# Five of nine positions of a q batch turned by DMA instead of TensorE, with their scaled values kept in other tiles

## The chip, the cores and the metric

The kernel runs on one core of one Trainium2 chip. The metric is device microseconds for one execution. The time shown for a kernel is the median of several runs.

## What is computed

Linear attention with cosine weights, followed by a gated feed-forward block. Cut to what matters:

```python
# q, k, v: (8 batches, 8 heads, 576 tokens, 64)
theta = pi / 2 * pos / 576
def phi(x): r = maximum(x, 0); return concatenate([r * cos(theta), r * sin(theta)], -1)
q_p, k_p = phi(q), phi(k)                       # last axis 128 wide
kv  = einsum('bhsf,bhsd->bhfd', k_p, v)
den = einsum('bhsf,bhf->bhs', q_p, k_p.sum(axis=2))[..., None] + 1e-6
x   = einsum('bhsf,bhfd->bhsd', q_p, kv) / den  # then to (4608 tokens, 512)
out = (gelu(x @ w_gate) * (x @ w_val)) @ w_out  # 512 -> 1536 -> 512
```

## The kernel before

**Tiling.** Batches are of 576 tokens, blocks of the feed-forward part of 512; nine blocks of tokens cover the eight batches. While TensorE works on the feed-forward matmuls of one block, the other engines and short insertions in TensorE's stream prepare the attention of the next batches. The order of instructions is written out by hand: each engine executes its instructions in the order of the program, and semaphores are placed where data or a buffer requires it.

**One batch of attention.** A batch is loaded as `qf`, `kf`, `vf` tiles (float32, two buffers each): 128 partitions are 2 heads of a pair times 64 groups of tokens, and each partition holds, for the four head pairs m, nine consecutive tokens, the positions j = 0 to 8 (`R = 9`). `prep` (L153) applies relu and the cosine (VectorE, L163) or the sine (ScalarE, L161) for one position over all four pairs and writes bf16 into the tile `qp` or `kp`. These have one buffer each, so batch 2's `qp` overwrites batch 1's. `cast_v` (L178) makes v bf16. `kv_unit` (L236) forms kv with 72 matmuls. q has to stand with its 128 features on the partitions before it can be multiplied with kv; that is the tile `qT`, one buffer. It is made in one of two ways:

- `turn_q_pe` (L201) with `turn_j` (L702): one TensorE transpose (L205) for each head pair and position, into a PSUM bank, and a copy from there to `qT` (L707, on ScalarE or VectorE). Batches 0 and 1 take this way.
- `turn_q` (L192): two DMA transposes from SP's queue (L194), one for each half of the partitions, 64 x 4608 elements each. Batches 2 to 7 take this way.

`nm_unit` (L274) then makes, for 128 tokens (a row tile t of five: t = 0 reads positions 0 and 1, t = 1 reads 2 and 3, t = 2 reads 4 and 5, t = 3 reads 6 and 7, t = 4 reads 7 and 8), eight matmuls of `qT` with kv (L283), the reciprocal and the division on VectorE (L294 to L296), which give `x_sb`. That is turned again (`turn_x_pe`, L354, TensorE transposes L358 and a ScalarE copy L362; or `turn_x` with DMA transposes L350) into `xT`, the input of the next block.

**The stage of the change.** It comes after block 0's 12 gate-and-value units (`gv_unit`, L401, with gelu on ScalarE L409 and the product on VectorE L410). During the last three of these, q of batch 1 is scaled: positions 0-2, 3-5 and 6-8. Then the list `order` (L773) mixes the output matmuls of block 0 (`o_part`, L431; four rows of tokens in three parts of four matmuls, with a ScalarE copy L440 and a store L421 from SP's queue at the end of each row) with batch 1's attention: turning q, scaling k ("k"), casting v ("q8" does this after the last transposes), kv, and the numerators "nm" for t = 0 to 3. "q2" scales the first positions of batch 2's q, on ScalarE first and then VectorE. After the list come the loads of batch 3's q from SP's queue. t = 4 of batch 1 follows in block 1 (about 60.5 us).

**Queues.** GpSimd's queue carries the loads of weights and of batches 1 and 2, all issued by 44.3 us; SP's queue carries stores, later loads and DMA transposes. SP's queue is empty between the loads at the start and the first store, issued at 51.74 us.

**Later weight sums.** `wo_sum` (L451) makes four differences of w_out's blocks, `T1` to `T4`, each in a tile of its own of 1536 bf16 columns (L459, L460). VectorE makes the first at 66.3 us.

Of the kernel before, what the change touches and what calls it, by code (L numbers as in the profile page):

```python
# [10 lines left out]
BF16 = mybir.dt.bfloat16  # L11
# [5 lines left out]
def kernel(  # L17
# [15 lines left out]
    B, H, S, D = q.shape  # L33
    F = 2 * D
    C = H * D
    J = moe_w_gate.shape[1]
    CT = C // 128
    JT = J // 128
    NP = H // 2
    R = S // 64  # L40
# [9 lines left out]
    weights = ctx.enter_context(tc.tile_pool(name="weights", bufs=1))  # L50
    inp = ctx.enter_context(tc.tile_pool(name="inp", bufs=2))
    attn = ctx.enter_context(tc.tile_pool(name="attn", bufs=1))
# [12 lines left out]
    def bank(i):  # L65
        return ps[:, i]

    def bank16(i):
        return ps[:, i].bitcast(BF16)
# [6 lines left out]
    staged = {}  # L76
# [54 lines left out]
    vx_tiles = []  # L131
    for i in range(2):
        t = consts.tile([128, NP, R, D + 1], BF16, name=f"vx{i}")
# [9 lines left out]
    act_copy, dve_copy = nc.scalar.copy, nc.vector.tensor_copy  # L143


    phi = {}

    def phi_tile(name, b):
        if (name, b) not in phi:
            phi[name, b] = attn.tile([128, NP, R, F], BF16, name=name + "p")  # L150
        return phi[name, b]

    def prep(name, b, part, js, m0=0, m1=NP, eng=None):  # L153
        dst = phi_tile(name, b)
        src = staged[name, b]
        tab = (cos_t, sin_t)[part]
        for j in js:
            o = dst[:, m0:m1, j, part * D:(part + 1) * D]
            i = src[:, m0:m1, j * D:(j + 1) * D]
            if eng is nc.scalar:  # L160
                nc.scalar.activation(o, i, AF.Relu, scale=tab[:, j:j + 1])  # L161
            else:
                (eng or nc.vector).tensor_scalar(  # L163
                    o, i, 0.0, tab[:, j:j + 1], op0=ALU.max, op1=ALU.mult
                )

    def prep_run(name, b, part, m, j0=0, j1=R):
        dst, src = phi_tile(name, b), staged[name, b]
        tab = (cos_t, sin_t)[part]
        nc.vector.scalar_tensor_tensor(  # L170
            dst[:, m, j0:j1, part * D:(part + 1) * D],
            src[:, m, j0 * D:j1 * D].rearrange("p (j d) -> p j d", d=D),
            0.0,
            tab[:, j0:j1, None].to_broadcast([128, j1 - j0, D]),
            op0=ALU.max,
            op1=ALU.mult,
        )

    def cast_v(b, m0, m1, copy, j0=0, j1=R):
        copy(  # L180
            vx_tiles[b % 2][:, m0:m1, j0:j1, 0:D],
            staged["v", b][:, m0:m1, j0 * D:j1 * D].rearrange("p m (j d) -> p m j d", d=D),
        )

    qT = {}

    def qt_tile(b):
        if b not in qT:
            qT[b] = attn.tile([128, 2, NP, R * 64], BF16, name="qT")
        return qT[b]  # L190

    def turn_q(b):  # L192
        for i in range(2):
            nc.sync.dma_start_transpose(  # L194
                out=qt_tile(b)[:, i].rearrange("f m (j p) -> f (m j) p", p=64),
                in_=phi["q", b][64 * i:64 * i + 64].rearrange("p m j f -> p (m j f)"),
            )

    def q_cols(b, t, h):
        c0 = min(t * 128, S - 128)  # L200
        return qT[b][:, h % 2, h // 2, c0:c0 + 128]  # L201

    def turn_q_pe(b, m, js, dst):
        for n, j in enumerate(js):
            nc.tensor.transpose(  # L205
                out=dst[:, n * 128:(n + 1) * 128],
                in_=phi["q", b][:, m, j, :],
                identity=ident,
            )

    kv_sb = {}

    def kv_pairs(b, m0, m1, banks):
        kp, vx = phi["k", b], vx_tiles[b % 2]
        for m in range(m0, m1):
            for j in range(R):
                for i in range(2):
                    rr = slice(64 * i, 64 * i + 64)
                    nc.tensor.matmul(
                        bank(banks[i])[:, (m % 2) * (D + 1):(m % 2 + 1) * (D + 1)],  # L220
                        lhsT=kp[rr, m, j, :],
                        rhs=vx[rr, m, j, :],
                        start=(j == 0),
                        stop=(j == R - 1),
                    )
# [8 lines left out]
            )  # L234

    def kv_unit(b):  # L236
        kp, vx = phi["k", b], vx_tiles[b % 2]
        for m in range(NP):
            for j in range(R):
                for i in range(2):  # L240
                    rr = slice(64 * i, 64 * i + 64)
                    nc.tensor.matmul(  # L242
                        bank(6 + i)[:, m * (D + 1):(m + 1) * (D + 1)],
                        lhsT=kp[rr, m, j, :],
                        rhs=vx[rr, m, j, :],
                        start=(j == 0),
                        stop=(j == R - 1),
                    )
        kv_sb[b] = attn2.tile([128, NP, 2, D + 1], BF16, name="kv_sb")
        for i in range(2):  # L250
            nc.scalar.copy(
                kv_sb[b][:, :, i, :],
                bank(6 + i)[:, 0:NP * (D + 1)].rearrange("p (m d) -> p m d", m=NP),
            )
# [99 lines left out]
    def turn_x_pe(b, t, to, copy):  # L354
        x = xs.pop((b, t))
        p = bank16(to)[:, 0:CT * 128].rearrange("p (c n) -> p c n", c=CT)
        for ct in range(CT):
            nc.tensor.transpose(  # L358
                out=p[:, ct, :], in_=x[:, ct * 128:(ct + 1) * 128], identity=ident
            )  # L360
        for blk, c, o, m in pieces(b, t):
            copy(xT_block(blk)[:, :, c:c + m], p[:, :, o:o + m])  # L362
# [86 lines left out]
    JH, CH = JT // 2, C // 2  # L449
    ts = {}  # L450

    def wo_sum(name):
        if not ts:
            ts["B11"], ts["B12"] = wo_sb[:, 0:JH, 0:CH], wo_sb[:, 0:JH, CH:C]
            ts["B21"], ts["B22"] = wo_sb[:, JH:JT, 0:CH], wo_sb[:, JH:JT, CH:C]
        x, y = {
            "T1": ("B12", "B11"), "T2": ("B22", "T1"), "T3": ("B22", "B12"), "T4": ("T2", "B21"),
        }[name]
        ts[name] = weights.tile([128, JH, CH], BF16, name=name)  # L459
        nc.vector.tensor_tensor(ts[name], ts[x], ts[y], op=ALU.subtract)  # L460

    def h_parts(n, p):
# [239 lines left out]
    def turn_j(b, m0, m1, js, to, copy):  # L702

        n = len(js)
        for m in range(m0, m1):
            turn_q_pe(b, m, js, bank16(to)[:, (m - m0) * n * 128:])
        copy(  # L707
            qt_tile(b)[:, :, m0:m1, js[0] * 64:(js[0] + n) * 64].rearrange(
                "f i m (j p) -> f m j i p", j=n
            ),  # L710
            bank16(to)[:, 0:(m1 - m0) * n * 128].rearrange(
                "f (m j i p) -> f m j i p", m=m1 - m0, j=n, i=2
            ),
        )
# [44 lines left out]
    for jt in range(4, JT):  # L759
# [12 lines left out]
    banks0 = (4, 5, 0, 1)  # L772
    order = (  # L773
# [6 lines left out]
    )  # L780
    for what, *a in order:
        if what == "o":
            o_part(a[0], range(a[1], a[1] + 4), banks0[a[0]], act_copy)
        if what == "q":
            turn_j(1, a[0], a[1], range(a[2], a[2] + 4), a[3], (dve_copy, act_copy)[a[3] % 2])
        if what == "q8":
            turn_j(1, 0, 4, (R - 1,), a[0], dve_copy)
            for m in (0, 2):
                cast_v(1, m, m + 2, dve_copy)
        if what == "k":  # L790
            prep("k", 1, 0, range(R))
            prep("k", 1, 1, range(7), eng=nc.scalar)
            prep("k", 1, 1, range(7, R))
        if what == "q2":
            prep("q", 2, 1, range(*a), eng=nc.scalar)
            prep("q", 2, 0, range(*a))
        if what == "kv":
            kv_unit(1)
        if what == "nm":
            nm_unit(1, a[0], a[1])  # L800
        if what == "xt":
            turn_x_pe(1, a[0], a[1], act_copy)
# [74 lines left out]
    for n in range(1, NB - 2):  # L877
        b = n + 1
# [4 lines left out]
        for jt in range(min(JT, FAST - n * JT)):  # L883
# [6 lines left out]
            else:  # L890
                for i in range(2):
                    half, unit = divmod(2 * jt + i, heads)
                    gv_unit(n, unit, half * HALF, HALF)
                    if n == 1:
                        j = JA + 2 * jt + i
# [4 lines left out]
            if n > 1:  # L900
                p, u = divmod(jt, 6)
# [6 lines left out]
            if b < B:  # L908
# [12 lines left out]
                i = jt - t_nm - 1  # L921
# [22 lines left out]
                c = {(2, 1): 2}.get((n, jt), b if n > 1 and jt == t_turn else None)  # L944
# [22 lines left out]
    for t in range(UNITS):  # L967
        n, jt = divmod(FAST + t, JT)
        if n == NB - 1 and jt in (9, 10):
            h_sum(n, jt - 9, "S3", eng=nc.gpsimd)  # L970
        if n < NB - 2:
# [3 lines left out]
            a, j0 = (("S2", 0), ("S4", 0), ("S2", 512), ("S4", 512))[t]  # L975
# [23 lines left out]
    for what in (  # L999
# [3 lines left out]
        if isinstance(what, str):  # L1003
            p = "ST".index(what[0])
# [33 lines left out]
```

## Time and profile before

| | us |
|---|---|
| median of 3 runs | 312.69 (312.32 to 313.81) |
| the profiled execution | 312.79 |
| its span | 311.0 |
| TensorE busy in the span | 301.0 |
| VectorE busy | 246.8 |
| ScalarE busy | 186.6 |
| last gate-and-value matmuls of block 0 end | 39.5 |
| batch 1's kv product starts | 47.7 |
| batch 1's numerators t = 0, 1, 2, 3 start | 49.8, 50.9, 52.3, 53.6 |
| block 1's first gate-and-value matmuls start | 55.0 |

The span is the time from the first to the last instruction of the profiled execution; the execution's own time has some 1.8 us around it. Times of single instructions are from the span's start. In the profile PE is TensorE, DVE VectorE, ACT ScalarE, POOL GpSimd and SP the engine that issues most DMAs; "idle before" is the time in which the engine stood, with what ended it.

### The profile page before, as it was taken

What the parts mean: (1) busy time and instruction counts of PE and PEld (TensorE: products, weight loads), DVE (VectorE), ACT (ScalarE), POOL (GpSimd) and SP (SyncE); (2) the same over time, 40 slices, a digit from 0 to 9 for tenths busy, and PEclk for the clock granted to TensorE, in tenths of its full rate; (3) what the DMA queues carried; (4) which work ended last, traced back from release to release, by engine and by line L of the source; (5) the groups of instructions that cost most, each with busy time, mean ns of one, the idle gap of its engine ahead of it and who ended that gap; (6) DMA issues with size and microseconds to landing.
All of it is one profiled execution on the core that took longest, in us unless ns stands there. A gap on an engine that the chain in (4) does not pass through costs nothing.

```text
span 311.0 us, 7704 instructions
## 1 busy us (share of the span) xinstructions
PE 301.0 (97%) x2867; PEld 208.2 (67%) x2895; DVE 246.8 (79%) x622; ACT 186.6 (60%) x468; POOL 67.9 (22%) x70
## 2 busy tenths in 40 slices
PE   8889999999999999999999999999999999999993
PEld 3574456645876676666666566656668888888882
DVE  5954686699897997799688878899899787978782
ACT  7854685966564763365525932593328787787830
POOL 6775420000000000000000000000007991297310
PEclk9999999999999999999999999999999999999999
DMA  7999999971798956993898589538442111202034
GB/s 277 247 186 246 313 315 412 273 145 37 217 225 260 315 132 153 368 232 94 259 291 177 116 277 303 112 83 124 93 106 52 40 32 41 50 21 69 3 80 123
DMA packets 69077, 53.65 MB, mean 172 GB/s; under 512 B 45392, under 2 KB 54352, under 8 KB 69040
## 3 DMA queue, kind: packets, MB, share of 16 engines
q1 hardware_dynamic: 59264, 41.17, 52.0%
q0 software_dynamic: 9696, 11.93, 16.5%
q8 instruction: 22, 0.36, 0.5%
q14 instruction: 15, 0.12, 0.1%
q10 hardware_dynamic: 80, 0.07, 0.1%
HBM read 37.75 MB, written 9.44 MB: 152 GB/s over the span
## 4 chain that ended last, share of the span: by engine, by line
PE 87%; DMA 4%; issue 4%; POOL 2%; DVE 0%; SPq 0%; ACT 0%; POOLq 0%; ACTq 0%; DVEq 0%
PE ps L401 43%; PE ps L510 20%; PE ps L611 13%; PE ps L431 3%; PE ps L283 3%; PE ps L242 3%; DMA vf<-in_v_dram 2%; DMA wv_sb<-in_moe_w_val_dram 2%; POOL kf L494 1%; PE ps L373 1%; PE ps L205 1%; PE ps L358 0%; SPq L81 0%; POOL gate L679 0%; POOL wg_sb L95 0%
## 5 line engine op out<-in xcount | busy, mean ns | idle before, releaser
L401 PE MATMUL ps<-xT,wv_sb 128*128 128x512 bf16 (+1 forms) x338 | 80.6, 359 | 0.2
L401 PE MATMUL ps<-xT,wg_sb 128*128 128x512 bf16 (+1 forms) x326 | 79.5, 358 | 1.1 <-issue 0.3
L409 ACT ACTIVATE gel<-ps 128x512 f32<-128x512 f32 (+1 forms) x86 | 47.7, 556 | 46.5 <-PE ps L401 43.3
L410 DVE TENSOR_TENSOR hT<-gel,ps 128x512 bf16<-128x512 f32 (+1 forms) x86 | 54.0, 633 | 24.0 <-PE ps L401 19.2
L401 PEld LDWEIGHTS <-wv_sb 128*128 128x128 bf16 x344 | 33.6, 98 | 33.9
L401 PEld LDWEIGHTS <-wg_sb 128*128 128x128 bf16 x344 | 30.7, 98 | 20.9 <-issue 0.2
L974 POOL CAST gate<-qp 128x1 f32<-128x1 bf16 x1 | 0.2, 175 | 190.7 <-DVE qp L591 190.7
L510 PEld LDWEIGHTS <-S 128*128 128x128 bf16 x336 | 32.9, 98 | 10.9 <-DVE S L494 0.6
L528 ACT COPY u<-ps 128x256 f32<-128x256 f32 x42 | 15.6, 372 | 31.4 <-PE ps L510 30.8
L510 PE MATMUL ps<-T,S 128*128 128x256 bf16 x252 | 34.4, 273 | 0.0
L161 ACT ACTIVATE qp<-qf,sin_t 128x256 bf16<-128x256 f32 x72 | 32.1, 502 | 3.4 <-DMA qf<-in_q_dram 3.4
L510 PEld LDWEIGHTS <-hT 128*128 128x128 bf16 x288 | 28.2, 98 | 6.9
L524 DVE TENSOR_TENSOR o_sb<-u,ps 128x256 f32<-128x256 f32 x56 | 23.3, 416 | 10.5 <-ACT u L528 10.3
L161 ACT ACTIVATE kp<-kf,sin_t 128x256 bf16<-128x256 f32 (+1 forms) x73 | 30.0, 480 | 0.9 <-DMA kf<-in_k_dram 0.9
L296 DVE TENSOR_TENSOR x_sb<-ps,rec 128x512 bf16<-128x512 f32 x38 | 26.3, 691 | 1.8 <-DMA xT<-x_sb 0.6
L510 PE MATMUL ps<-wo_sb,hT 128*128 128x256 bf16 x192 | 23.7, 273 | 0.0
L163 DVE TENSOR_SCALAR qp<-qf,cos_t 128x256 bf16<-128x256 f32 x71 | 21.5, 350 | 2.3 <-DMA qf<-in_q_dram 2.3
L611 PE MATMUL ps<-qp,qf 128*128 128x256 bf16 x112 | 21.4, 273 | 0.1
L611 PE MATMUL ps<-xT,wg_sb 128*128 128x256 bf16 x112 | 21.4, 273 | 0.0
L163 DVE TENSOR_SCALAR kp<-kf,cos_t 128x256 bf16<-128x256 f32 x63 | 18.3, 347 | 0.0
L283 PEld LDWEIGHTS <-qT 128*128 128x128 bf16 x304 | 14.6, 98 | 2.7 <-ACT qT L707 0.3
L283 PE MATMUL ps<-kv_sb,qT 128*128 128x65 bf16 x304 | 16.0, 194 | 0.0
(121 smaller groups left out, 457.6 us busy)
## 6 DMA issues: line engine op xcount, KB each, us to landing
out_dram<-o_sb SPq DMA_DIRECT2D x69, 128.0 KB, 2.5
kf<-in_k_dram SPq DMA_DIRECT2D x12, 576.0 KB, 7.2
vf<-in_v_dram SPq DMA_DIRECT2D x12, 576.0 KB, 9.0
qf<-in_q_dram SPq DMA_DIRECT2D x10, 576.0 KB, 5.2
qf<-in_q_dram POOLq DMA_DIRECT2D x4, 576.0 KB, 12.1
kf<-in_k_dram POOLq DMA_DIRECT2D x4, 576.0 KB, 12.8
vf<-in_v_dram POOLq DMA_DIRECT2D x4, 576.0 KB, 12.9
wg_sb<-in_moe_w_gate_dram POOLq DMA_DIRECT2D x6, 256.0 KB, 6.9
```

The costliest lines, as they stand in the source:

```text
L161: nc.scalar.activation(o, i, AF.Relu, scale=tab[:, j:j + 1])
L163: (eng or nc.vector).tensor_scalar(o, i, 0.0, tab[:, j:j + 1], op0=ALU.max, op1=ALU.mult)
L242: nc.tensor.matmul(bank(6 + i)[:, m * (D + 1):(m + 1) * (D + 1)], lhsT=kp[rr, m, j, :], rhs=vx[rr, m, j, :], start=(j == 0), stop=(j == R ...
L283: nc.tensor.matmul(bank(b0 + h // 4)[:, (h % 4) * (D + 1):(h % 4 + 1) * (D + 1)], lhsT=q_cols(b, t, h), rhs=kv_sb[b][:, h // 2, h % 2, :], ...
L296: nc.vector.tensor_tensor(x, nm[:, :, :, 0:D], rec[:, :, :, None].to_broadcast([128, 2, 4, D]), op=ALU.mult,)
L401: nc.tensor.matmul(bank(b0 + g)[:, 0:w], lhsT=wt[:, ct, js], rhs=xt[:, ct, c0:c0 + w], start=(ct == 0), stop=(ct == CT - 1),)
L409: nc.scalar.activation(gel[:, 0:w], bank(b0)[:, 0:w], AF.Gelu)
L410: nc.vector.tensor_mul(hT[n][:, jt, c0:c0 + w], gel[:, 0:w], bank(b0 + 1)[:, 0:w])
L510: nc.tensor.matmul(at, lhsT=hs.setdefault(key, h_parts(n, p))[a][:, j], rhs=ts[b][:, j], start=(j == 0 and i in (1, 2, 4, 5)), stop=(j == ...
L524: nc.vector.tensor_tensor(o, got[key, k], x, op=op)
L528: nc.scalar.copy(got[key, i], at)
L611: nc.tensor.matmul(at(i, t), lhsT=wa[a][:, ct, jt * 128:(jt + 1) * 128], rhs=xb[n][b][:, ct], start=(ct == 0 and i in (1, 5)), stop=(ct == ...
```

## The change

Positions 4 to 8 of batch 1's q leave the TensorE way. Their scaled values no longer go to `qp` but into two extra tiles: positions 4 and 5 into one with the name `T1`, positions 6 to 8 into one with the name `T2`, so that they take the places in which two of w_out's differences are made later. Four DMA transposes (two halves for each of the two parts) are issued from SP's queue ahead of the list; 20 TensorE transposes and three copies leave it. Batch 1's `qT` is laid out in three parts (positions 0-3, 4-5, 6-8), so that each transfer writes one run. The casts of v stand in the list where the last transposes stood, and one of the two halves goes to ScalarE. The diff, cut to its core:

```diff
+    JB, JC = 4, 6
+    def parted(flat, n, b, name="q"):
+        ends = (0, JB, JC, R) if (name, b) == ("q", 1) else (0, R)
+        return [
+            (j0, flat[:, j0 * NP * n:j1 * NP * n].rearrange(
+                "p (m j n) -> p m j n", m=NP, j=j1 - j0))
+            for j0, j1 in zip(ends, ends[1:])
+        ]
+    def at_j(parts, j):
+        j0, t = [part for part in parts if part[0] <= j][-1]
+        return t, j - j0
     def phi_tile(name, b):
         if (name, b) not in phi:
-            phi[name, b] = attn.tile([128, NP, R, F], BF16, name=name + "p")
+            t = attn.tile([128, NP, R, F], BF16, name=name + "p")
+            phi[name, b] = parted(t.rearrange("p m j f -> p (m j f)"), F, b, name)
+            if (name, b) == ("q", 1):
+                for i, (j0, j1) in enumerate(((JB, JC), (JC, R))):
+                    t = weights.tile([128, JT // 2 * C // 2], BF16, name=f"T{i + 1}")
+                    phi[name, b][1 + i] = j0, t[:, 0:NP * (j1 - j0) * F].rearrange(
+                        "p (m j f) -> p m j f", m=NP, j=j1 - j0
+                    )
...
-    def turn_q(b):
+    def turn_q(b, part=0):
         for i in range(2):
             nc.sync.dma_start_transpose(
-                out=qt_tile(b)[:, i].rearrange("f m (j p) -> f (m j) p", p=64),
-                in_=phi["q", b][64 * i:64 * i + 64].rearrange("p m j f -> p (m j f)"),
+                out=qt_tile(b)[i][part][1].rearrange("f m j p -> f (m j) p"),
+                in_=phi["q", b][part][1][64 * i:64 * i + 64].rearrange("p m j f -> p (m j f)"),
             )
     def q_cols(b, t, h):
-        c0 = min(t * 128, S - 128)
-        return qT[b][:, h % 2, h // 2, c0:c0 + 128]
+        cols, j = at_j(qT[b][h % 2], min(2 * t, R - 2))
+        return cols[:, h // 2, j:j + 2].rearrange("f j p -> f (j p)")
...
     order = (
         [("q", 0, 2, 0, 6), ("q", 2, 4, 0, 7), ("o", 0, 0), ("k",), ("o", 1, 0)]
-        + [("q", 0, 2, 4, 2), ("o", 2, 0), ("q", 2, 4, 4, 3), ("o", 3, 0), ("o", 0, 4)]
-        + [("q8", 2), ("o", 1, 4), ("o", 2, 4), ("kv",), ("q2", 0, 2), ("o", 3, 4)]
+        + [("o", 2, 0), ("o", 3, 0), ("o", 0, 4)]
+        + [("v",), ("o", 1, 4), ("o", 2, 4), ("kv",), ("q2", 0, 2), ("o", 3, 4)]
...
+    turn_q(1, 1)
+    turn_q(1, 2)
     for what, *a in order:
...
-        if what == "q8":
-            turn_j(1, 0, 4, (R - 1,), a[0], dve_copy)
-            for m in (0, 2):
-                cast_v(1, m, m + 2, dve_copy)
+        if what == "v":
+            for m, copy in ((0, dve_copy), (2, act_copy)):
+                cast_v(1, m, m + 2, copy)
```

More of the change, by code (lines that the diff above doesn't have):

```diff
@@ L157, in prep @@
         for j in js:
-            o = dst[:, m0:m1, j, part * D:(part + 1) * D]
+            t, jj = at_j(dst, j)
+            o = t[:, m0:m1, jj, part * D:(part + 1) * D]
             i = src[:, m0:m1, j * D:(j + 1) * D]
@@ L167, in prep_run @@
     def prep_run(name, b, part, m, j0=0, j1=R):
-        dst, src = phi_tile(name, b), staged[name, b]
+        (_, dst), = phi_tile(name, b)
+        src = staged[name, b]
         tab = (cos_t, sin_t)[part]
@@ L183, in cast_v @@
         )
-    qT = {}
+    qT, first = {}, {}
     def qt_tile(b):
         if b not in qT:
-            qT[b] = attn.tile([128, 2, NP, R * 64], BF16, name="qT")
+            t = attn.tile([128, 2, NP * R * 64], BF16, name="qT")
+            qT[b] = [parted(t[:, i], 64, b) for i in range(2)]
+            n = qT[b][0][0][1].shape[2]
+            first[b] = t[:, :, 0:NP * n * 64].rearrange(
+                "f i (m j p) -> f i m j p", m=NP, j=n
+            )
         return qT[b]
-    def turn_q(b):
+    def turn_q(b, part=0):
         for i in range(2):
             nc.sync.dma_start_transpose(
-                out=qt_tile(b)[:, i].rearrange("f m (j p) -> f (m j) p", p=64),
-                in_=phi["q", b][64 * i:64 * i + 64].rearrange("p m j f -> p (m j f)"),
+                out=qt_tile(b)[i][part][1].rearrange("f m j p -> f (m j) p"),
+                in_=phi["q", b][part][1][64 * i:64 * i + 64].rearrange("p m j f -> p (m j f)"),
             )
     def q_cols(b, t, h):
-        c0 = min(t * 128, S - 128)
-        return qT[b][:, h % 2, h // 2, c0:c0 + 128]
+        cols, j = at_j(qT[b][h % 2], min(2 * t, R - 2))
+        return cols[:, h // 2, j:j + 2].rearrange("f j p -> f (j p)")
     def turn_q_pe(b, m, js, dst):
@@ L206, in turn_q_pe @@
                 out=dst[:, n * 128:(n + 1) * 128],
-                in_=phi["q", b][:, m, j, :],
+                in_=phi["q", b][0][1][:, m, j, :],
                 identity=ident,
@@ L213, in kv_pairs @@
     def kv_pairs(b, m0, m1, banks):
-        kp, vx = phi["k", b], vx_tiles[b % 2]
+        kp, vx = phi["k", b][0][1], vx_tiles[b % 2]
         for m in range(m0, m1):
@@ L236, in kv_unit @@
     def kv_unit(b):
-        kp, vx = phi["k", b], vx_tiles[b % 2]
+        kp, vx = phi["k", b][0][1], vx_tiles[b % 2]
         for m in range(NP):
@@ L458, in wo_sum @@
         }[name]
-        ts[name] = weights.tile([128, JH, CH], BF16, name=name)
+        t = weights.tile([128, JH * CH], BF16, name=name)
+        ts[name] = t.rearrange("p (j c) -> p j c", j=JH)
         nc.vector.tensor_tensor(ts[name], ts[x], ts[y], op=ALU.subtract)
@@ L706, in turn_j @@
             turn_q_pe(b, m, js, bank16(to)[:, (m - m0) * n * 128:])
+        qt_tile(b)
         copy(
-            qt_tile(b)[:, :, m0:m1, js[0] * 64:(js[0] + n) * 64].rearrange(
-                "f i m (j p) -> f m j i p", j=n
-            ),
+            first[b][:, :, m0:m1, js[0]:js[0] + n].rearrange("f i m j p -> f m j i p"),
             bank16(to)[:, 0:(m1 - m0) * n * 128].rearrange(
```

## The prediction

> **What bounds the kernel now.** I read the page first, then the TensorE timeline around the change, then ScalarE and VectorE in the same stretch, then the DMA queues.
>
> ```profile
> PE 301.0 (97%) x2867; PEld 208.2 (67%) x2895; DVE 246.8 (79%) x622; ACT 186.6 (60%) x468; POOL 67.9 (22%) x70
> ...
> DMA  7999999971798956993898589538442111202034
> ```
>
> TensorE is busy 97% of the span, and the chain that ended last is 87% TensorE. So what leaves its stream in front of the end shortens the kernel, and a wait put into that stream lengthens it. The second line is the mean busy share of the DMA engines in slices of 7.8 us: 9 tenths from 8 to 62 us. The change sits at 39 to 54 us, inside that full stretch.
>
> ```profile
> 39.52 1.06 PE L205 MATMUL ps<-ident,qp 128*128 128x128 bf16 x16
> ...
> 42.14 0.61 PE L205 MATMUL ps<-ident,qp 128*128 128x128 bf16 x8
> ...
> 43.45 0.61 PE L205 MATMUL ps<-ident,qp 128*128 128x128 bf16 x8
> ...
> 45.62 0.39 PE L205 MATMUL ps<-ident,qp 128*128 128x128 bf16 x4
> ...
> 47.67 1.33 PE L242 MATMUL ps<-vx,kp 64*128 64x65 bf16 x72
> ...
> 52.05 0.39 PE L358 MATMUL ps<-ident,x_sb 128*128 128x128 bf16 x4
> 52.27 0.42 PE L283 MATMUL ps<-kv_sb,qT 128*128 128x65 bf16 x8
> ...
> 53.62 0.42 PE L283 MATMUL ps<-kv_sb,qT 128*128 128x65 bf16 x8
> ```
>
> Start, duration, instruction. The first row stays (positions 0 to 3), the next three are what is removed; the fifth is the kv product, the sixth the turning of batch 1's first output rows. The last two are the numerators of batch 1's third and fourth row tile (t=2, t=3), which read positions 4-5 and 6-7.
>
> ```profile
> 49.03 0.66 ACT L251 CAST kv_sb<-ps 128x260 bf16<-128x260 f32 x2 [3.72 <-PE ps L242]
> ...
> 50.14 0.91 ACT L161 ACTIVATE qp<-qf,sin_t 128x256 bf16<-128x256 f32 x2 [0.45 <-DMA qf<-in_q_dram]
> ...
> 51.13 0.58 ACT L440 COPY o_sb<-ps 128x512 f32<-128x512 f32 x1
> ...
> 50.16 0.62 DVE L163 TENSOR_SCALAR qp<-qf,cos_t 128x256 bf16<-128x256 f32 x2 [2.35 <-DMA qf<-in_q_dram]
> ```
>
> Here batch 2's first scalings wait, on ScalarE and on VectorE, for batch 2's q from memory: its second half was issued at 36.40 and landed 13.6 us later, at 50.0. They do not wait for TensorE's last reading of qp, which ended by 46.0.
>
> ```profile
> q0 software_dynamic: 207, 0.84, 102.5%
> ...
> q0 software_dynamic: 40, 0.15, 60.2%
> q1 hardware_dynamic: 44, 0.08, 37.3%
> ...
> DMA packets 695, 0.18 MB, mean 178 GB/s; under 512 B 695, under 2 KB 695, under 8 KB 695
> ...
> q1 hardware_dynamic: 695, 0.18, 84.6%
> ```
>
> The DMA queues (packets, MB, share of 16 engines) in three windows. From 48 to 50 us GpSimd's loads alone fill all engines. From 53.6 to 54.2 SP's first stores run beside them: 44 packets against 40, though SP had by then issued some three stores of 80 packets: a turn each, whatever the size. From 64 to 65 a q transpose runs alone: its packets are 256 bytes (0.18 MB in 695), and one costs an engine 0.846 us x 16 / 695 = 19.5 ns.
>
> ```profile
> L194 SPq DMA_TRANSPOSE qT<-qp x12: 3673/3754/3914, 61.9 to 208.4; - x12
> ...
> L350 SPq DMA_TRANSPOSE xT<-x_sb x34: 1187/1252/3425, 69.7 to 233.2; - x34
> ```
>
> Minimum, median and maximum ns of SP's issue of the two kinds of transpose, for 2304 and 512 packets.
>
> **What the Trainium skill says.** "DMA: Bandwidth & Descriptors", section "Queues, rings and completion order": each DMA engine goes round-robin between its queues at packet granularity. The 44-to-40 window agrees; that a transpose's packet is 256 bytes for this purpose, no window here shows under contention. The same page, "Issuing engines are not separate DMA queues": DMAs of SP and GpSimd share the same 16 engines, which the same window shows. "VectorE: DVE Perf Modes", "The three transpose paths": 390 ns for TensorE's 128x128 transpose, 1309 ns for the DMA's; in this trace TensorE's are pipelined, 16 in 0.89 us, so the saving is 55 ns each. "TensorE: Matmul & The Clock Gate", "HAM oscillation": idle gaps of TensorE over about 3.4 us bring the half clock back; no gap of that length is in this trace, but the 22 opening matmuls take 7.25 us, 330 ns each, where later ones start every 216 ns, so a cold start cost 2.5 us.
>
> **The change, part by part.**
>
> *Removed from TensorE:* 8 + 8 + 4 transposes. In the stream of starts they take 0.45, 0.45 and 0.23 us (42.14 to 42.59, 43.45 to 43.90, 45.62 to 45.85): 1.13 us, all on the path. This is the cap of the gain; the stretch has only 0.2 us of TensorE gaps besides. *Removed copies:* 0.68 + 0.42 us VectorE, 0.99 us ScalarE; neither ended a TensorE wait there, so nothing.
>
> *Moved cast of v:* one half goes from VectorE (0.755 us) to ScalarE. ScalarE's row is not shown for that size; from its copies of 512 and 1024 columns (0.59 and 1.0 us) I estimate 1.1 us. That half of v lands at 44.7 (issued 30.99, 13.7 us). With the 0.5 us of delay worked out below, it is cast by 46.3; the kv product, now starting at 47.67 - 1.13 = 46.54, reads it at 47.2. Covered by 0.9 us; if v came 1 us later still, it would cost 0.1 us.
>
> *Other views of the same scalings (L161, L163):* the same 18 instructions with other strides, nothing either way. *Weight sums in T1 and T2:* the first starts at 66.3; it waits for the transposes to have read, 7 us earlier even below. Nothing. *SP:* four transposes. From 512 packets in 1.22 us and 2304 in 3.74, 1.4 ns a packet on 0.5: 1.22 us for each of the two of positions 4-5 (512 packets), 1.58 us for each of positions 6-8 (768). The first can start at 39.6 when those positions are scaled, the rest at 41.2; SP is done at 45.2. Its next work, the stores, starts at 51.74, so its issuing costs nothing. The stores' packets queue behind the transposes on q1, but o_sb has four buffers and the next products come at 80 us.
>
> *The wait that is added:* TensorE waits for the transposes to land before t=2 and t=3, and all TensorE work queues behind it in order. When do they land? From 41.2 each engine still has, by the landings of the eight half loads and two weight loads before and behind it, 7 packets of the second third of w_out, 16 of v, 32 of w_out's last third (78 ns each), and 48 of q, k and v of batch 2 (8 per half load, 175 ns each): 103, the last at 55.7. The transposes bring 32 + 32 + 48 + 48 = 160 packets per engine. One turn each, at 20 ns: positions 4-5 (64 packets) get through with the first 64 of the loads, which before were over at 48.8; plus 64 x 20 ns, 50.1, and about 0.5 to signal. In time for t=2. Positions 6-8: by the end of the loads at 55.7 + 103 x 0.02 = 57.8 only 103 of 160 have gone; the other 57 take 1.1 us alone: 58.9. I take 58.6 (issue at 39.6 instead of 41.2 helps a few), with the signal 59.1.
>
> *What is late next:* batch 2's q. 71 load packets stand before its end, so 71 x 20 ns = 1.4 us: 51.4 instead of 50.0. ScalarE's sines and the copy of the first output (L440, ended 51.7) move with it, and the transposes at 52.05 use that copy's bank. Without the change to DMA they would go at 51.75, as soon as the copy ends: of the 1.13 us, 0.3 would be left. With it they go at 53.1, and t=3 is ready at 54.7. It then waits to 59.1.
>
> *Sum:* t=3 at 59.1 instead of 53.6: +5.5 us, with the 1.13 and the 1.4 inside it. Profiled execution 312.79 (span 311.0 and 1.8 around it) gives 318.3; the median shown is 0.1 lower: **318.2**. Ends: 17 ns a packet gives +4.9; 39 ns (the first microsecond of a transpose, 512 packets at 124.6%) gives +8.5; a cold clock after a gap of 4 us could add up to 2.
>
> **The rivals.**
>
> *Transposes go in large turns.* If an engine sends some 16 of these packets per turn, they go as fast as SP issues and land by 47.5; t=3 finds them. Then all 160 go ahead of batch 2's q: 160 x 17 to 25 ns = 2.7 to 4.0 us later, less the 0.3: +2.4 to +3.7, 315.2 to 316.4. For: the rate alone (170 GB/s) is set by SP. Against: the packets are recorded singly, and singly recorded stores took turns singly.
>
> *Hidden (not slower).* The DMA engines carry 0.66 MB more (160 x 16 x 256 bytes) without delaying the loads, because a transpose's writes inside the chip use what loads from memory leave idle; positions 6-8 land before 53.3. Then the q load at 50.0 bounds, and the gain is 0.3 to 1.13 us: 311.6 to 312.4. It decides from the point where batch 2's q lands within 0.3 us of 50.0. The stated purpose gives nothing more, since batch 2 waits for its load and not for qp. Against: a busy share of 102% in that window.
>
> *False order.* If the copies of positions 0-3 into qT had to wait for the transposes into the same tile, VectorE and ScalarE would stand from 41 to 59: 325 and more. Against: before, two copies into that tile (ScalarE 40.61, VectorE 41.19) overlap.
>
> **How the numbers follow.** The range is 312.0 to 321.5. One turn each: 0.50, own range 316.5 to 321.5. Large turns: 0.25. Hidden: 0.20. False order: 0.05. The low end takes in the large turns and the upper half of the hidden case, the high end the 39 ns packets; left out are the false order, the lower half of hidden and the cold clock on top: 2 in 10. About 0.5% (1.6 us) is what a measurement of this kernel tells from no change. The cap of 1.13 us plus gaps leaves faster by more only 0.03; the hidden case gives 0.19 and the best large turns 0.03 for within, so 0.22; slower 0.75.
>
> **What would show it.** Right: a TensorE gap before the t=3 numerator of 3 to 6 us that ends with the DMA of qT; transposes of positions 6-8 landing 12 us or more after issue; q0 and q1 with like packet counts at 42 to 55 us; batch 2's q at about 51.4. Large turns: qT lands before 49, the gap is before the transposes at 52 and ends with the ScalarE copy behind the q load. Wrong altogether: no TensorE gap over 0.5 us in 45 to 60.

## The result, and the profile after

| | median us | ratio to before |
|---|---|---|
| before | 313.25 (6 runs) | |
| after | 322.57 (321.35 to 322.94, 6 runs) | 1.0295, 95% interval 1.027 to 1.0321 |

Times and ratios, here and below, leave out the two runs that were disturbed (327.77 and 328.89 us, in two of the experiments), and ratios can differ a little from those of the medians. The change makes the kernel 9.3 us slower. The forecast was 318.2 with a range up to 321.5: the direction held, the size did not. In the profiled executions the span grows from 311.0 to 320.9 us.

First the page of the kernel after: the busy line of TensorE, and the clock granted to it by slices of 8 us.

```profile
PE 305.5 (95%) x2875; PEld 208.9 (65%) x2875; DVE 245.5 (77%) x619; ACT 187.5 (58%) x468; POOL 67.8 (21%) x70
...
PEclk9999999589999999999999999999999999999998
```

TensorE is busy 4.5 us longer than before although 20 transposes left it. The second line says where most of it comes from: in the eighth slice, 56 to 64 us, it ran at half clock. From the stretch's first transposes to t=4 it is busy 24.4 us instead of 20.7. Another 0.8 us is counted in a hundred microseconds further on (99.2 and 100.0 us), where the trace of before has 15 matmul records fewer (927 and 942), so that part may be no work. Next TensorE's timeline of the kernel after (start, duration, instruction, and in brackets the idle time ahead of it with what ended it).

```profile
46.38 1.43 PE L272 MATMUL ps<-vx,kp 64*128 64x65 bf16 x72
...
49.77 1.02 PE L461 MATMUL ps<-wo_sb,hT 128*128 128x512 bf16 x4 [0.73 <-DMA wo_sb<-in_moe_w_out_dram]
...
54.62 0.40 PE L388 MATMUL ps<-ident,x_sb 128*128 128x128 bf16 x4 [2.71 <-DVE x_sb L326]
...
56.10 0.49 PE L313 MATMUL ps<-kv_sb,qT 128*128 128x65 bf16 x7 [1.06 <-DMA qT<-T]
...
60.69 0.24 PE L313 MATMUL ps<-kv_sb,qT 128*128 128x65 bf16 x1 [1.97 <-DMA qT<-T]
61.31 0.56 PE L313 MATMUL ps<-kv_sb,qT 128*128 128x65 bf16 x7 [0.38 <-DMA qT<-T]
```

The kv product starts at 46.38 instead of 47.67: the saving of the 20 transposes is there. Then come five waits: for w_out's last third, ahead of turning batch 1's first output, ahead of t=2, and two ahead of t=3, which has its data at 61.31; before, it started at 53.62. ScalarE and VectorE in the same stretch:

```profile
52.89 0.91 ACT L185 ACTIVATE qp<-qf,sin_t 128x256 bf16<-128x256 f32 x2 [4.40 <-DMA qf<-in_q_dram]
...
52.91 0.62 DVE L187 TENSOR_SCALAR qp<-qf,cos_t 128x256 bf16<-128x256 f32 x2 [7.46 <-DMA qf<-in_q_dram]
```

Batch 2's q lands at 52.8 instead of 50.0, and the waits for it are 4.40 and 7.46 us instead of 0.45 and 2.35. Now the DMA queues of the kernel after (packets, MB, share of the 16 engines) from 48 to 53 us, and SP's four transposes:

```profile
q0 software_dynamic: 442, 1.78, 109.0%
q1 hardware_dynamic: 442, 0.11, 10.5%
...
L224 SPq DMA_TRANSPOSE qT<-T x4: 1273/3726/8591, 39.6 to 48.5; - x4
...
DMA to landing us min/median/max: 9.5/13.9/18.3
```

In five microseconds 442 packets of GpSimd's loads went and 442 packets of the transposes: turn for turn, 4 KB against 256 bytes. A transpose of 2304 packets landed 5.4 us after its issue when alone (65.70 to 71.08 before); these, of 512 and 768 packets, take 9.5 to 18.3 us. SP itself was held, up to 8.6 us in one issue: its four transposes took from 39.6 to 57.1 us.

Added up from the profiled executions, by TensorE's starts:

| stretch | before | after | difference |
|---|---|---|---|
| transposes of positions 0-3 to t=3 (last seven matmuls of it after) | 39.52 to 53.62 | 39.35 to 61.31 | +7.86 |
| t=3 to t=4 | 53.62 to 60.53 | 61.31 to 70.55 | +2.33 |
| t=4 to the end of the span | 250.5 | 250.35 | -0.1 |

The whole loss lies before 71 us and nothing of it comes back. (The stretch itself starts 0.17 us earlier after.)

### The profile page after: what moved, and what is told of

It is laid out like the page before. It is cut to its first block, busy times and chain, and to the rows that moved or that the text cites. A ratio compares the mean times of both kernels' runs of the same rounds, so it can differ in the third digit from the quotient of the medians.

```text
span 320.9 us, 7693 instructions
## 1 busy us (share of the span) xinstructions
PE 305.5 (95%) x2875; PEld 208.9 (65%) x2875; DVE 245.5 (77%) x619; ACT 187.5 (58%) x468; POOL 67.8 (21%) x70
## 4 chain that ended last, share of the span: by engine, by line
PE 85%; DMA 7%; issue 3%; DVE 1%; POOL 1%; SPq 1%; ACT 1%; POOLq 0%; ACTq 0%; DVEq 0%
PE ps L431 43%; PE ps L541 19%; PE ps L642 12%; DMA qT<-T 4%; PE ps L313 3%; PE ps L272 3%; DMA vf<-in_v_dram 3%; PE ps L461 2%; POOL kf L525 1%; PE ps L403 1%; PE ps L235 1%; PE ps L388 1%; SPq L81 1%; DVE vx L205 0%; DVE x_sb L326 0%
## 5 line engine op out<-in xcount | busy, mean ns | idle before, releaser
L431 PE MATMUL ps<-xT,wg_sb 128*128 128x512 bf16 (+1 forms) x344 | 82.2, 362 | 0.0
L431 PE MATMUL ps<-xT,wv_sb 128*128 128x512 bf16 (+1 forms) x344 | 81.9, 361 | 0.0
L431 PEld LDWEIGHTS <-wg_sb 128*128 128x128 bf16 x344 | 31.2, 99 | 20.7
L185 ACT ACTIVATE qp<-qf,sin_t 128x256 bf16<-128x256 f32 x67 | 29.7, 499 | 7.9 <-DMA qf<-in_q_dram 7.9
L187 DVE TENSOR_SCALAR qp<-qf,cos_t 128x256 bf16<-128x256 f32 x66 | 20.3, 353 | 7.7 <-DMA qf<-in_q_dram 7.7
```

The costliest lines, as they stand in the source:

```text
L187: (eng or nc.vector).tensor_scalar(o, i, 0.0, tab[:, j:j + 1], op0=ALU.max, op1=ALU.mult)
L431: nc.tensor.matmul(bank(b0 + g)[:, 0:w], lhsT=wt[:, ct, js], rhs=xt[:, ct, c0:c0 + w], start=(ct == 0), stop=(ct == CT - 1),)
```

## The experiments

Theory ("turns"): a DMA engine alternates between its queues by packet, so the transposes get one packet of 256 bytes per load packet; TensorE stands until they land, and the half clock follows. Rivals: "late q" (most of the loss is batch 2's q, which the transposes delay and which holds ScalarE and VectorE), and "own rate" (these small transposes are slow by themselves). All edits are to the kernel after, except where the kernel before is named.

**TensorE turns all positions again, the DMA transposes go to unread places.**

```diff
-    turn_q(1, 1)
-    turn_q(1, 2)
+    for part, (j0, j1) in ((1, (JB, JC)), (2, (JC, R))):
+        to = weights.tile([128, 2, NP * (j1 - j0) * 64], BF16, name=f"T{part + 2}")
+        for i in range(2):
+            nc.sync.dma_start_transpose(
+                out=to[:, i].rearrange("f (m p) -> f m p", p=64),
+                in_=phi["q", 1][part][1][64 * i:64 * i + 64].rearrange("p m j f -> p (m j f)"),
+            )
...
```

> TensorE turns all nine positions again, as before; the four DMA transposes run as in the change but write into the later places of T3 and T4, which nobody reads. Turns theory (a transpose gets one 256-byte packet through per load packet, and the loss is mostly TensorE's waiting for them): only the delay of the loads is left, batch 2's q at 52.8 instead of 50.0, so +2 to +3.5 us, 315 to 317. Late-q theory (the loss is mostly batch 2's late q, which holds ScalarE and VectorE): nearly the whole loss stays, 320 or more. Own-rate theory (the small transposes are slow by themselves and load nothing else): 313 to 314.

Measured: 316.47, ratio 1.0101 (1.0053 to 1.015), as the turns theory had it. The traffic alone, without TensorE's wait for it, costs about 3 us. TensorE's timeline of this run shows one wait in the stretch, ahead of turning the first output; VectorE, which makes that output, had stood 5.49 us for batch 2's q, landed at 53.18:

```profile
55.02 0.40 PE L385 MATMUL ps<-ident,x_sb 128*128 128x128 bf16 x4 [2.13 <-DVE x_sb L323]
```

So about a third of the loss stays when TensorE doesn't wait for the transposes, and in this profile most of it is late q. Late q as the cause of most of the loss (320 or more) falls, and so does own rate, which had the traffic cost nothing.

**The same, with batch 2's q scaled only after t=2 and t=3** (the entries "q2" of the list moved).

> As the run with TensorE turning all positions and the DMA transposes writing into unread places, and batch 2's q is scaled only after t=2 and t=3. If the 2.9 us of that run are batch 2's late q holding ScalarE and VectorE in order: they go, 313 to 314. If they come from something else that the transposes slow (w_out's last third, the stores): 315.5 to 317.

Measured: 315.57, ratio 1.0068 (1.004 to 1.0097), just inside the second expectation, and 0.9 us below the run ahead of it, with intervals that overlap. In its profiled execution (313.91 us, the fastest of its six) TensorE's starts from 39.51 to 54.74 agree with those of before to 0.01 us, so the wait for batch 2's q is gone there. A new gap of 0.58 us ahead of block 1's units stands behind a ScalarE copy; why the other five runs take 314.80 to 316.19 us is not accounted for. So that late q makes up all of the 3 us is not shown.

**In the change, only batch 2's q scaled after the last numerator.**

```diff
-        + [("v",), ("o", 1, 4), ("o", 2, 4), ("kv",), ("q2", 0, 2), ("o", 3, 4)]
+        + [("v",), ("o", 1, 4), ("o", 2, 4), ("kv",), ("o", 3, 4)]
...
-        + [("xt", 2, 4)]
+        + [("xt", 2, 4), ("q2", 0, 2), ("q2", 2, 3), ("q2", 3, 4)]
```

> The change with one edit: batch 2's q is scaled after the last numerator, so its late landing holds nobody ahead of t=3. Turns theory: t=2 and t=3 still wait for the transposes to land, near 56 and 61.2, the half clock follows as before; 321.5 to 323.5. Late-q theory: the loss falls by its 2.5 to 3 us, 319 to 320.

Measured: 323.03, ratio 1.028 (1.0244 to 1.0315). TensorE's timeline of this run:

```profile
59.68 0.57 PE L313 MATMUL ps<-kv_sb,qT 128*128 128x65 bf16 x7 [7.65 <-DMA qT<-T]
```

With batch 2's q out of the way nearly all the waiting gathers at the transposes, here of positions 4-5, ahead of t=2. t=3 starts 21.97 us after the stretch's first transposes (40.20 to 62.17), in the change 21.96. So late q is refuted as the cause: in the change it is covered by the longer wait. The later scaling has a price of its own, a wait of 1.49 us in block 1.

**The loads of batch 2's k and v held until the transposes have landed**, by a copy on GpSimd that reads the last of them; in one run alone, in one with the later scaling too.

```diff
-    for name in ("q", "k"):
-        for m in (0, 2):
-            load(nc.gpsimd, name, 2, m, m + 2)
     for m in (0, 2):
-        load(nc.gpsimd, "v", 2, m, m + 2)
+        load(nc.gpsimd, "q", 2, m, m + 2)
...
     turn_q(1, 2)
+    nc.gpsimd.tensor_copy(gate2, qT[1][1][2][1][:, 0, 0, 0:1])
+    for m in (0, 2):
+        load(nc.gpsimd, "k", 2, m, m + 2)
+    for m in (0, 2):
+        load(nc.gpsimd, "v", 2, m, m + 2)
```

> Only the loads of batch 2's k and v wait for the last transpose; the scalings of batch 2's q stay where the change has them. Turns theory: the transposes land as in the run that also moved those scalings, the last near 54.7, and batch 2's q at 51 to 51.5 (as before plus some 70 turns of 20 ns); the gap ahead of turning the first output is 1 us, and t=3 starts near 55 instead of 61: 314 to 315.5. If instead the place of the scalings made that run fast and not the held loads: t=3 stays near 61 and the time near 322.

Measured: 316.62, ratio 1.0111 (1.0086 to 1.0137). t=3 starts at 55.61, near what was expected; the time is 1.1 us above the range. In the profile batch 2's q came at 51.8, and the gap of 2.82 us ahead of the first output was followed by a low clock (0.80 from 53 to 56 us, 0.64 from 56 to 59): from t=3 to t=4 it takes 8.02 us instead of 6.91.

> The loads of batch 2's k and v wait for the last transpose to land, and the scalings of batch 2's q move behind the last numerator, so that neither the later loads compete nor the late q holds ScalarE and VectorE. Turns theory: about 56 load packets stand before the transposes from 43.3 us on, up to 50.5; the other 104 go alone at 20 to 39 ns, and the last lands at 53 to 55 instead of 61.2; with no half clock the time is 312.5 to 316. Own-rate theory: the last lands at 59 or later, 320 or more. Late-q theory: about 313, but with the transposes still landing after 58.

Measured: 315.94, ratio 1.0076 (1.0046 to 1.0106). TensorE's timeline of this run:

```profile
54.66 0.40 PE L313 MATMUL ps<-kv_sb,qT 128*128 128x65 bf16 x7 [1.41 <-DMA qT<-T]
...
59.62 0.60 PE L431 MATMUL ps<-xT,wg_sb 128*128 128x256 bf16 x4 [1.50 <-ACT xT L392]
```

Without 32 load packets per engine (four half loads of 8) the last transpose lands 6.6 us earlier (54.62 instead of 61.26), and t=3 has its data at 54.66. The second line is the price of the later scaling: four sines stand ahead of a copy that block 1 needs.

**All loads of batch 2 held.**

> All loads of batch 2 (q, k and v) wait for the last transpose, and batch 2's q is scaled after the last numerator. Turns theory: from 43.3 us only some 40 load packets stand in the queue, over by 48; the rest of the transposes go alone and the last lands at 50.5 to 52.5, before t=3 wants it at 52.7, so no wait of TensorE there is left; what is lost is batch 2's q, which lands near 56 and is scaled late: 313.5 to 316.5. Own-rate theory: t=3 still waits past 55.

Measured: 319.3, ratio 1.016 (1.0128 to 1.0191). Its DMA queues from 48 to 50 us carried nearly nothing but transposes, 823 and 712 packets a microsecond, where the change had 78 and 90, and t=3 went at 52.08 without a wait: what the turns theory says of a queue with few load packets left, and the end of own rate. The time was missed, since batch 2's q, whose loads were held as well, landed 3.6 us later than I had put it (59.6) and its sines stood ahead of the same copy: TensorE waited 6.76 us there.

**Only positions 6 to 8 by DMA.**

```diff
-        ends = (0, JB, JC, R) if (name, b) == ("q", 1) else (0, R)
+        ends = (0, JC, R) if (name, b) == ("q", 1) else (0, R)
...
-        + [("o", 2, 0), ("o", 3, 0), ("o", 0, 4)]
+        + [("o", 2, 0), ("q45", 2), ("o", 3, 0), ("o", 0, 4)]
```

> Only positions 6 to 8 go by DMA (96 packets per engine instead of 160); TensorE turns 0 to 5, and batch 2's q keeps the change's places. Turns theory: the first transpose packets go near 43.3, some 88 load packets stand in the queue from there, so nearly all 96 go with them and the last lands near 58; t=2 waits for nothing, t=3 starts near 58.3: 317 to 319.5. By-bytes sharing or a fixed rate (96/160 of the time from issue to landing of the change, 13 us): landed by 54.5, 315 to 316.

Measured: 321.09, ratio 1.0225 (1.0189 to 1.0262): above the turns theory's figure and far above a fixed rate or sharing by bytes. 96 packets instead of 160 leave three quarters of the loss. The first packet went at 44.9, not 43.3, and t=3 had its data at 60.16. From that first packet on only 58 load packets per engine were still to go, not 88, the last at 59.1; the transposes' 96 outlast them turn for turn, and their last went at 59.6. So the alternation holds, and what the expectation had wrong is when the loads end. TensorE had also stood 4.18 us ahead of turning the first output, for batch 2's q, without making t=3 later.

**Transposes out of qp instead of the extra places** (the six lines that allocate `T1` and `T2` left out).

> The change without its extra places: positions 4 to 8 are scaled into qp as before, and the DMA transposes read them there, so batch 2's scalings must wait for the transposes to land, at 61 us. Turns theory: ScalarE stands at batch 2's first sines until the last transpose has read, near 61, then copies the first output; TensorE stands ahead of turning it, and t=2, t=3 come after: 4 to 8 us slower than the change, 326 to 331. If the places do nothing (batch 2 waits for its load anyway): 322 to 323.

Measured: 325.72, ratio 1.0403 (1.0383 to 1.0423), just below the range of the turns theory. The waits of this run (total us, times, longest):

```profile
DVE qp L180 <- DMA qT<-qp: 16.0, 1, 16.0
ACT qp L178 <- DMA qT<-qp: 13.1, 1, 13.1
```

So the extra places do what they are for: without them ScalarE and VectorE wait 13.1 and 16.0 us for the transposes before they can scale batch 2's q, and the kernel loses 3 us more. It is a wait that the change itself brings; before, no such wait existed.

**Matmuls on zeros in the waits**, once in the change, once with the later scaling.

```diff
         if what == "nm":
+            if a[0] == 2:
+                dummies(6, 2)
+            if a[0] == 3:
+                dummies(16, 6)
             nm_unit(1, a[0], a[1])
```

> 6 matmuls on zeros ahead of t=2 and 16 ahead of t=3 keep TensorE busy for 1.3 and 3.5 us of its waits; nothing else changes. If the half clock from 56 to 66 us cost what lies behind the last wait (4.7 us of work at half speed, so 2.3 us), the time falls by 2 to 2.5 us to about 320.3. If the low clock is only a reading and not a cost, it stays at 322.6, or rises by what the added matmuls delay.

Measured: 321.1, ratio 1.0243 (1.0198 to 1.0287). From t=3 to t=4 it takes 6.86 us (63.03 to 69.89), as before (6.91), instead of 9.24; t=3 came 0.4 us later by the stretch's own start. So in the profiles the half clock costs 2.3 us after the last wait, and about 2 can be had back. The ratio's gain, 1.6 us, is near that and below the 2 to 2.5 expected, and its interval overlaps that of the change.

> As the run that only scales batch 2's q late, and 20 matmuls on zeros (4.3 us at full clock) ahead of t=2 and 20 ahead of t=3 fill TensorE's two waits. If the half clock after the waits costs 2 to 2.5 us: that much faster than the run without them, 319.5 to 321, with TensorE at full clock throughout. If it costs nothing: the same or slower by up to 1 us, where the added matmuls outlast the wait.

Measured: 322.14, ratio 1.0259 (1.0218 to 1.0299), against 323.03 without: less than expected. Without them the wait was one, and the low clock ended at 64 us on its own. The windows from 55 to 60 and from 60 to 65 us, without and then with the added matmuls (length, TensorE busy with its instructions, granted clock, share of the DMA engines, GB/s):

```profile
55.00:60.00 5.00, 0.32 (x7) 0.72 1.28 208
60.00:65.00 5.00, 4.78 (x34) 0.60 0.57 170
```

```profile
55.00:60.00 5.00, 4.72 (x32) 1.00 1.23 269
60.00:65.00 5.00, 5.00 (x45) 1.00 1.00 331
```

The clock is full with them; from t=3 to t=4 they save 0.9 us (9.31 to 8.44), as much as the medians differ, though the intervals overlap.

**Batch 2's loads split into 12 transfers of one head pair.**

```diff
-    for name in ("q", "k"):
-        for m in (0, 2):
-            load(nc.gpsimd, name, 2, m, m + 2)
-    for m in (0, 2):
-        load(nc.gpsimd, "v", 2, m, m + 2)
+    for name in ("q", "k", "v"):
+        for m in range(NP):
+            load(nc.gpsimd, name, 2, m, m + 1)
```

> Batch 2's q, k and v are loaded in 12 transfers of one head pair instead of 6 of two, so that their packets are half as large and twice as many, at the same bytes. Turns theory: twice as many turns for the transposes in that stretch; the second transpose of positions 4-5 lands near 52 instead of 56, the last near 57 instead of 61, and the time falls to 316 to 319. If the engines share by bytes, or if the transposes are slow by themselves: landings and time as in the change, 322 to 323.

Measured: 329.97, ratio 1.051 (1.0478 to 1.0542): a miss, and its premise failed too. The packets did not shrink: they have 4608 bytes as before (from 48 to 49 us, 102 packets of 3.6 KB in the mean, with small signalling ones among them). And from 52 to 66 us both queues crept; its queues from 55 to 56 us:

```profile
q1 hardware_dynamic: 100, 0.02, 116.9%
q0 software_dynamic: 21, 0.08, 34.0%
```

> The kernel before, with batch 2's q, k and v in 12 transfers of one head pair. If the split loads creep by themselves: loads still moving at 65 us at under 150 GB/s, batch 2's kv late, 316 to 325. If only beside transposes: loads over by 57 us at 400 GB/s, 313 to 314.5.

This is the kernel before with the same split loads. Measured: 313.55, ratio 1.0002 (0.9986 to 1.0019), the loads landed by 56.5 us, as expected. So the split alone costs nothing; in these runs loads and transposes creep only together, and only when the loads are split. A reading that fits: a transpose's packets on the idle engines wait for those on the engines that still have loads, and so all go at the slowest one's pace. The counts are sums over the engines, so this is argued, not shown, and it doesn't say why the split matters.

**A candidate**: positions 4 to 8 scaled first, k and v held, batch 2's q scaled behind t=2 and t=3, two output parts ahead of the first transposes.

```diff
-    q1 = {9: (0, 1, 2), 10: (3, 4, 5), 11: (6, 7, 8)}
+    q1 = {9: (4, 5, 6), 10: (7, 8, 0), 11: (1, 2, 3)}
...
-        [("q", 0, 2, 0, 6), ("q", 2, 4, 0, 7), ("o", 0, 0), ("k",), ("o", 1, 0)]
+        [("o", 0, 0), ("o", 1, 0), ("k",), ("q", 0, 2, 0, 6), ("q", 2, 4, 0, 7)]
```

> Candidate for a version that pays: positions 4 to 8 are scaled ahead of 0 to 3, so that the transposes start some 1.5 us earlier, batch 2's k and v are held as in the runs before, its q is scaled after t=2 and t=3, and the turning of positions 0 to 3 comes after two output parts. Turns theory: the last transpose lands near 53, t=3 wants it near 52.7; 312.5 to 314.5. If the DMA engines are simply full until 54 whatever the order: 315 to 316.

Measured: 314.43 (12 runs), ratio 1.0039 (1.0016 to 1.0062): within its expected range, the best form of the idea, and still 0.4% behind the kernel before. t=2 waits 0.71 us for positions 4-5, t=3 not at all.

## Why the prediction was wrong, point by point

**Right: what bounds, the cap, the mechanism.** The saving of TensorE is the 1.13 us: kv product less start of the stretch, 47.67 - 39.52 = 8.15 before, 46.38 - 39.35 = 7.03 after. The two queues sent as many packets each. The transposes of positions 6-8 and batch 2's q came late, and TensorE's waits ahead of turning the first output and ahead of t=3 are where the prediction put them. Two waits it did not have: 0.73 us for w_out's last third, and 1.06 us ahead of t=2, for positions 4-5, which it called "in time for t=2" at about 50.6 and which landed at 56.06. The rival "large turns" falls with the 442 against 442, "false order" with the copies of positions 0 to 3 at 40.45 and 41.12, "hidden" with the result.

**Wrong by size, first term: "I take 58.6 ... with the signal 59.1."** Measured 61.3, 2.2 us later. The step that failed is the one that counts the turns from 41.2 and puts 20 ns on each. The transposes' packets began at 43.5, 3.9 us after the first issue (3.8 to 3.9 in all the runs here with these transposes); alone, a transpose's first packet goes 1.3 us after issue (61.89 to 63.19 before), and the working counted from 1.6 us after the first. By 57 us 1192 of their 2560 packets of 256 bytes had gone, where the working had 103 of 160 per engine, so 1648, by 57.8. And the loads were at their end 4.5 us later than before, where 103 turns of 20 ns make 2.1. Their landings show where:

| landed at, us | before | after | later by |
|---|---|---|---|
| w_out's second third | 41.90 | 42.38 | 0.48 |
| batch 1's v, second half | 44.69 | 45.83 | 1.14 |
| w_out's last third | 47.22 | 49.73 | 2.51 |
| batch 2's q, second half | 50.03 | 52.78 | 2.75 |
| batch 2's k, first half | 51.44 | 55.88 | 4.44 |
| batch 2's v, second half | 55.67 | 60.18 | 4.51 |

The first row's half microsecond was there before any packet of a transpose had gone, so it is not their doing. Most of the rest comes beside w_out's packets of 1 KB and, ahead of batch 2's k, in a standstill of both queues of about 1 us (19 packets in all from 53 to 54). From k's first half to the end of the loads another 24 turns went by, and they cost 0.07 us. A like lull, of 7 to 68 packets in one microsecond, recurs in seven of the other runs, but not in the four that held batch 2's k and v while transposes were under way; its cause stays open. The tail does not go at 20 ns either: from 57 to 60 us 792 packets went at 97% of the engines' time, 59 ns each, beside 120 load packets. Why stays open too.

**Wrong by size, second term: the price of a packet for batch 2's q.** 20 ns, read from a transpose alone, holds as a packet's own time beside loads of q, k and v (10.4% of 16 engines for 92 packets from 50 to 51 us: 18 ns), but not beside w_out's: 39.6% for 109 packets from 44 to 45 us, 58 ns. So batch 2's q was 2.8 us late, not 1.4, and 2.5 of these were there when w_out's last third landed. That third, whose reader I had not followed, also held TensorE for 0.73 us. In the change the longer wait ahead of t=3 covers both, and the wait ahead of t=2 as well. That these errors don't show in the total is luck.

**Left out of the sum: the half clock.** The text had "a cold clock after a gap of 4 us could add up to 2" and left it out of value and range. It came, and cost 2.3 us. The section "HAM oscillation" of the Trainium skill's "TensorE: Matmul & The Clock Gate" gives 3.4 us as the idle time that matters; here shorter gaps were enough: 2.71 us, a few instructions and 1.06 us more in the change, one gap of 2.69 us in the change with matmuls on zeros, one of 2.82 us in the run with k and v held. A gap of 2.13 us in the run with unread places left the clock at 0.998. The measurement decides: one gap of 2.7 us can do it.

How the idle time falls counts as well. In these profiles full and half clock last whole steps of 3.41 us (in the change half from 56.24 to 66.48, three steps). From 45 to 75 us the clock fell after steps in which TensorE idled 2.08 us or more (2.85 in the change, 2.27 with k and v held, 2.08 with the transposes out of qp) and stayed full after those with 1.73 or less (1.73 with only the later scaling; 1.4 with unread places, where the gap lay across two steps). This is no bound for other stretches: near the start of one run a step with 1.45 us idle was followed by half clock.

With the 2.2 us of the landing these 2.3 us make up the 4.4 by which the forecast fell short of the profiled execution (318.3 against 322.72).

**Covers that were gone without cost.** SP's issuing, put at 5.6 us, took 17.5 and moved the first store from 51.74 to 57.22; nobody waited for it. The cast on ScalarE took 1.15 us (estimate 1.1) but waited 1.6 us for v, which landed at 45.83 instead of 44.69, and the kv product grew by 0.1 us.

## What to carry to other kernels

Where DMA engines are full, ask how many packets stand ahead and of what size, not how many bytes are added: a DMA transpose got one of its 256-byte packets through per packet of the loads (442 against 442), so one with many packets lands only when those loads are through or nearly so. Moving work from a full TensorE to a full DMA can pay only if the competing loads can wait, and then the saving (here 1.13 us) has to outweigh what those loads feed; in no run here did it. A wait put into TensorE's stream should be priced with the low clock that can follow it: here after gaps of 2.7 us and more, at a cost of 2.3 us in the change.

## What the runs showed of the hardware that was not expected

- SP was held in issuing while its packets went slowly: 8.6 us for one transpose of 768 packets, and 3.25 us for the same one with all loads of batch 2 held.
- Loads split so that each brings half the bytes kept packets of the same size, 4608 bytes.
- Beside the split loads, transposes went at about 100 packets a microsecond and loads at about 20 for some 10 us, while the same loads without transposes were unaffected (313.55 us, ratio 1.0002).
- The granted clock changed only in steps of 3.41 us, and gaps of TensorE well below that length were followed by half clock.
